# Last weight transposes moved to the score banks, and three low halves of the first expert's weights made by GpSimd

## The chip, the cores and the metric

The kernel runs on one core of one Trainium2 chip. The metric is the time of one execution on the device, in microseconds (us); lower is better.

## The reference

```python
def _attn_ref(q, k, v):              # q, k, v: (4, 8, 768, 64)
    block, window = (32, 16)
    k_sum = k.reshape(B, H, nb, block, D).max(axis=3)
    v_sum = v.reshape(B, H, nb, block, D).mean(axis=3)
    scores_l = scale * np.matmul(q, k.transpose(0, 1, 3, 2))
    mask_l = np.abs(pos[:, None] - pos[None, :]) < window
    scores_s = scale * np.einsum('bhsd,bhnd->bhsn', q, k_sum) + np.log(block)
    ...
    a = softmax over [masked local scores, block scores]
    return np.matmul(a, v_all)

def _moe_ref(x, w_group, w_expert, w1, w2):   # 3072 tokens of 512; 4 groups of 4 experts, hidden 1024
    g_idx = np.argmax(x @ w_group, axis=1)
    ...
        e_idx = np.argmax(xg @ w_expert[g], axis=1)
        ...
            h = np.maximum(xg[mask_e] @ w1[g, e], 0.0)
            ye = h @ w2[g, e]
            out[tok_idx] = combined[:, None] * ye
```

Local attention with block summaries is followed by a mixture of 16 experts, in which each token goes to one expert of one group.

## The kernel before

**Attention.** The 4 batches of 8 heads are 16 pairs of heads; each pair is cut into three groups of four blocks of 128 queries, which makes 48 groups (numbers 0 to 47 below). `attention()` steps through n = 0 to 50 and at each n issues, in the order that the table `PLAN` writes out, one piece of several groups at once: the scores of group n into two of the three score banks (`ps_s`), VectorE's masking and row minimum, ScalarE's exponentials ("e"), the transposes of the weights of group n - 2 (`transpose_p`, "t") with ScalarE's copy `ptS`, and the product with the values of group n - 3 (`values`, "v") into the one bank `ps_av`, which VectorE divides by the row sums into `x`. Steps "l0" to "l3" (`logits`) transpose x into `xT` and multiply it by the router's weights. Transposes of all kinds share the three banks `ps_tr` in turn.

**Routing.** `Router` works out which expert is largest and which of its tokens go first; its VectorE operations are fed into the stream between the others (`advance`). For the last batch but one they run at n = 48, in one piece: mx, dd, c, ..., seen. ScalarE takes one exponential, dd, from them.

**Experts.** Each product is made of three matmuls in a rounded fp32 format: high x high, low x high, high x low, where the high half is a rounding copy by ScalarE and the low half is a subtraction. `split_w` makes these halves of 128 x 1024 pieces; the four pieces (parts) of w1 of the first expert are split in the last steps of attention by `hook`. `hook` also gathers the first tokens (`gather1`), transposes them into high and low halves at n = 47 (`x_t1`), and advances `first`, whose stage 1 (`stage1_2`) writes hidden units into the score banks, two blocks of 128 to a bank; it takes two steps at n = 49 and one at n = 50 and n = 51, so stage 1 and the last steps of attention stand in each other's midst. Part p of w1 is first used by the p-th pair of hidden blocks.

Every engine runs its instructions in the order in which they were issued, GpSimd's queue with its gathers included. What is written out by hand here is that order: `SPLIT_AT` gives the step n, counted from 48, at which ScalarE's high half of each part is issued, and the low half follows one step later.

Of the kernel before, what the change touches and what calls it, by code (L numbers as in the profile page):

```python
# [8 lines left out]
F32 = mybir.dt.float32  # L9
# [5 lines left out]
ALU = mybir.AluOpType  # L15
# [40 lines left out]
T_LAG, V_LAG = 2, 3  # L56
# [6 lines left out]

W1_AT = 34
GATHER_AT, X_AT = 4, 1
SPLIT_AT = (-4, -3, -2, -1)
FIRST = {1: 2, 2: 1, 3: 1}

XT_AT = 4
# [5 lines left out]
class Banks:  # L75
# [5 lines left out]
    def next(self):  # L81
        self.n += 1
        return self.tiles[(self.n - 1) % len(self.tiles)]
# [506 lines left out]
def attention(tc, q, k, v, w_group, w_expert, ident, x_dram, ps, router, hook):  # L590
    nc = tc.nc
# [18 lines left out]
    V = nc.vector  # L610
    T = router.T
    ps_tr, ps_s, ps_av, ps_lg = ps["tr"], ps["s"], ps["av"], ps["lg"]
    lg = router.lg

    with ExitStack() as st, ExitStack() as nat_st:
# [6 lines left out]
        order = [(b, a) for b in range(B) for a in range(NP)]  # L622
# [36 lines left out]
        def keep_warm(n):  # L659
            t = ps_lg.next()  # L660
            for _ in range(n):
                nc.tensor.matmul(out=t, lhsT=zero, rhs=zero[:, None, :].broadcast_to([P, 4, P]), start=True, stop=True)  # L662
# [138 lines left out]
        def exps(n, sp, nm):  # L801
            pr = prr[n % 3]
            for i in range(4):
                nc.scalar.activation(out=pr[:, i, 0:NC], in_=sp[:, i], func=AF.Exp, bias=nm[:, i:i + 1], scale=-1.0)  # L804
            return pr

        def transpose_p(pr):
            pt = ps_tr.next()
            for i in range(4):
                T.transpose(out=pt[0:NR, i * P:(i + 1) * P], in_=pr[:, i], identity=ident)  # L810
            ptS = wk.tile([NR, 4, P], F32, name="ptS", bufs=3)
            nc.scalar.copy(out=ptS.rearrange("p a c -> p (a c)"), in_=pt[0:NR])
            return ptS
# [20 lines left out]
        def store():  # L834
            b, js = stores.pop(0)
            nc.sync.dma_start(out=x_dram[b * S:(b + 1) * S].rearrange("(j r) d -> r j d", r=P)[:, js], in_=xs[b][:, js])

        def logits(idx, part):
            b, a = order[idx]
            x = xs[b]  # L840
            if part < 2:
                if part == 0:
                    xTs[idx] = wk.tile([P, TB, P], F32, name="xT")
                j0, n = ((0, 4), (4, 2))[part]
                tp = ps_tr.next()
                for i in range(n):
                    T.transpose(out=tp[:, i * P:(i + 1) * P], in_=x[:, j0 + i, a * P:(a + 1) * P], identity=ident)
                (V.tensor_copy if part and idx < len(order) - 1 else nc.scalar.copy)(
                    out=xTs[idx][:, j0:j0 + n].rearrange("p c r -> p (c r)"), in_=tp[:, 0:n * P])
            elif part == 2:  # L850

                if a == 0:
                    lgp[b] = ps_lg.next()
                xT = xTs.pop(idx)
                for i in range(4):
                    rows = slice(32 * i, 32 * i + 32)
                    T.matmul(out=lgp[b][rows, 0:TB * 32], lhsT=wcat[:, a], rhs=xT[:, :, rows],
                             start=(a == 0), stop=(a == NP - 1), skip_group_check=True)
                if a == NP - 1:
                    lT = lgp["lT"] = sm.tile([P, TB * 32], F32, name="lT", bufs=1)  # L860
                    nc.scalar.copy(out=lT, in_=lgp.pop(b)[:, 0:TB * 32])
            elif a == NP - 1:
                tl = sm.tile([P, TB, 32], F32, name="tl", bufs=1)
                V.transpose(out=tl.rearrange("p t c -> p (t c)"), in_=lgp.pop("lT"))
                V.tensor_copy(out=lg[:, b * TB:(b + 1) * TB], in_=tl[:, :, 0:20])  # L865
                stores.extend((b, slice(j, j + 2)) for j in range(0, TB, 2))
# [4 lines left out]
        NG = 3 * len(order)  # L871
        prs, pts = {}, {}
# [14 lines left out]
        for n in range(NG + 3):  # L887
            idx, g = n // 3, n % 3
            if n < NG:
                b, a = order[idx]  # L890
                xs[b] = x_ring[b % 2]
            for step in START[n] if n < len(START) else PLAN[g]:
                if step == "s" and n < NG:
                    sps = scores(n)
                elif step == "e" and n < NG:
                    prs[n] = exps(n, *sps)
                elif step == "t" and 0 <= n - T_LAG < NG:
                    pts[n - T_LAG] = transpose_p(prs.pop(n - T_LAG))
                elif step == "v" and 0 <= n - V_LAG < NG:
                    values((n - V_LAG) // 3, (n - V_LAG) % 3, pts.pop(n - V_LAG))  # L900
                elif step[0] == "p" and n < NG and idx + 1 < len(order):
                    prep(idx + 1, int(step[1]))
                elif step[0] == "m" and n < NG:
                    j = idx + (step == "m0" and n > 2)
                    if (j > 0 or n < 3) and j < len(order):
                        means(j, int(step[1]))
                elif step == "w":
                    keep_warm(4)
                elif step == "n0":
                    means(1, 0)  # L910
                elif step[0] == "l" and 0 <= idx - LAG[step] < len(order):
                    logits(idx - LAG[step], int(step[1]))
            if n == 0:
                router.consts()
            elif n == 4:
                router.compared()
            if n in ROUTE_AT:
                b1 = ROUTE_AT.index(n)
                work.append(router.route(b1 * TB, (b1 + 1) * TB))
                if b1 == 1:  # L920
                    work.append(router.first_blocks())
            if n == NG - 4:
                nat_st.close()
            if n < NG:
                if g == 0 and idx + 2 < len(order):
                    load_vw(idx + 2)
                if g == 0 and idx < len(order) - 3:
                    qk[idx + 3] = load_qk(idx + 3)
            if g == 1 and stores:
                store()  # L930
            while stores and n == NG - 5:
                store()
            clock.step += 1
            hook(n, need, advance, w1_first)
# [11 lines left out]
class Experts:  # L946
# [76 lines left out]
    def split_w(self, row, which, parts, low=True, high=True):  # L1023

        raw = self.raw(row, which)
        for c in parts:
            js = slice(2 * c, 2 * c + 2)
            if which == 0:
                src = raw.rearrange("p c (j r) -> p c j r", j=FC)[:, :, js]
                h, l = (t[:, :, js] for t in self.w1s)  # L1030
            else:
                src = raw[:, js]
                h, l = (t[:, js] for t in self.w2s)
            if high:
                self.nc.scalar.copy(out=h, in_=src)  # L1035
            if low:
                self.V.tensor_tensor(out=l, in0=src, in1=h.bitcast(F32), op=ALU.subtract)

    def gather(self, row, dst, half=0):
        name, c = self.col(row, half)  # L1040
# [299 lines left out]
def block_attention_then_moe(tc, q, k, v, w_group, w_expert, w1, w2, out):  # L1340
    nc = tc.nc
    with ExitStack() as st:
# [12 lines left out]
        last = 3 * B * NP  # L1355

        first = ex.first()

        def hook(n, need, advance, space):

            if not ex.w1r and n >= W1_AT and (router.ready & 1 or n == last - 4):
                need(1)
                ex.w1r["first"] = space
                ex.load_w(("first", 0), 0)
            if n == last - 4:
                ex.tiles(st.enter_context(tc.tile_pool(name="m_w", bufs=1, side="right")), True)
            if n == last - GATHER_AT:
                need(2)
                ex.gather1(0)
                ex.load_w(("first", 0), 1, queue=nc.gpsimd)  # L1370
            if n == last - X_AT:
                ex.x_t1()
                if NE > 2:
                    ex.gather1(2)
            for part in range(4):
                if n == last + SPLIT_AT[part] + 1:
                    ex.split_w(("first", 0), 0, [part], high=False)
                if n == last + SPLIT_AT[part]:
                    ex.split_w(("first", 0), 0, [part], low=False)
            if n == last:  # L1380
                router.ahead = LATE_AHEAD
                advance(99)
            for _ in range(FIRST.get(n - last, 0)):
                next(first)
            if n > last + 1:
                advance(2 if n == last + 2 else 99)
# [3 lines left out]
        late = st.enter_context(tc.tile_pool(name="m_late", bufs=1))  # L1390
# [58 lines left out]
```

## Time and profile before

| | |
|---|---|
| median of 3 runs | 517.19 us (516.53 to 517.81) |
| profiled execution, own time | 515.85 us |
| its span, first to last instruction | 514.2 us |
| busy: TensorE matmul (PE) | 492.2 us, 96% |
| busy: TensorE weight load (PEld) | 415.5 us, 81% |
| busy: VectorE (DVE) | 356.6 us, 69% |
| busy: ScalarE (ACT) | 317.8 us, 62% |
| busy: GpSimd (POOL) | 120.9 us, 24% |

The profile is of one execution; its times count from the span's start. Busy shares are means over the whole span, and the seam that the change works on is only some 15 us of it, so the table says little of it: the rows below do.

### The profile page before, as it was taken

How to read it: one execution, taken by the hardware profiler on the slowest of the kernel's cores; microseconds unless marked ns; L12 is line 12 of the kernel's file. 1: busy time of each engine (PE TensorE's matmuls, PEld its weight loads, DVE VectorE, ACT ScalarE, POOL GpSimd, SP SyncE). 2: the span in 40 equal slices, each digit the busy share in tenths (PEclk: the TensorE clock that was granted, in tenths of full speed). 3: DMA queues.
4: the chain of work that ended last, by engine and by line, in shares of the span. 5: the costliest groups of instructions: out<-in, count | busy, mean ns of one | idle time of the engine just before them, and what ended most of it. 6: DMA issues, size and time to landing. Idle time of an engine off the chain costs nothing.

```text
span 514.2 us, 13346 instructions
## 1 busy us (share of the span) xinstructions
PE 492.2 (96%) x4974; PEld 415.5 (81%) x4974; DVE 356.6 (69%) x1084; ACT 317.8 (62%) x597; POOL 120.9 (24%) x205
## 2 busy tenths in 40 slices
PE   8999999999999899999999999999999999999994
PEld 4677767776777698979898989898898989897773
DVE  6687899888977978878755647483836556473773
ACT  5699888888988643216644556473645546474682
POOL 6122112211312600037020203022121202022332
PEclk9799999999999899999999999999999999999998
DMA  9999676879646820069997665665566756754891
GB/s 179 176 181 198 130 168 189 180 155 195 173 113 224 281 90 22 28 220 354 409 403 273 238 229 211 247 225 190 205 211 239 263 212 222 258 191 137 300 359 42
DMA packets 75316, 106.94 MB, mean 208 GB/s; under 512 B 40286, under 2 KB 40366, under 8 KB 75232
## 3 DMA queue, kind: packets, MB, share of 16 engines
q1 hardware_dynamic: 69184, 86.78, 58.5%
q0 software_dynamic: 6048, 19.12, 10.4%
q8 instruction: 43, 0.70, 0.6%
q14 instruction: 41, 0.34, 0.2%
HBM read 97.49 MB, written 13.24 MB: 215 GB/s over the span
## 4 chain that ended last, share of the span: by engine, by line
PE 49%; issue 19%; DMA 12%; DVE 11%; ACT 3%; POOL 3%; POOLq 1%; DVEq 0%; ACTq 0%
PE ps_s L122 26%; DMA out_dram<-y,t_unit_scatter 12%; PE ps_tr L122 12%; PE ps_av L122 10%; DVE ss L795 3%; DVE ks L775 2%; DVE kw L764 1%; ACT kw L764 1%; PE ps_lg L122 1%; POOL ohr L1042 1%; ACT qt L758 1%; PE ps_lg L662 1%; POOLq L1185 1%; ACT pr L804 1%; DVE kw L778 1%
## 5 line engine op out<-in xcount | busy, mean ns | idle before, releaser
L122 DVE TENSOR_TENSOR w2l<-w2r,w2h 128x1024 fp32r<-128x1024 f32 x52 | 63.4, 1225 | 77.1 <-ACT w2h L1035 76.6
L122 PE MATMUL ps_s<-xT,w1h 128*128 128x256 f32 x448 | 83.5, 284 | 0.0
L122 PEld LDWEIGHTS ps_s<-xT,w1h 128*128 128x128 f32 x448 | 70.7, 192 | 1.0 <-issue 0.7
L1082 POOL DMA_INDIRECT out_dram<-y,t_unit_scatter x24 | 25.7, 1069 | 190.9 <-ACT y L1077 97.7
L738 POOL COPY va<-vr 25x256 f32<-25x256 f32 x96 | 35.9, 418 | 118.8 <-DVE vr L735 118.8
L122 PE MATMUL ps_s<-xT,w1l 128*128 128x256 f32 x224 | 63.4, 283 | 0.0
L122 DVE TENSOR_TENSOR w1l<-w1r,w1h 128x1024 fp32r<-128x1024 f32 x52 | 60.4, 1219 | 3.6 <-ACT w1h L1035 3.6
L804 ACT ACTIVATE pr<-ss,nm 128x120 f32<-128x120 f32 x192 | 60.1, 387 | 3.3 <-DVE nm L795 2.9
L1120 ACT ACTIVATE hTh<-ps_s 128x512 fp32r<-128x512 f32 x48 | 28.7, 598 | 53.9 <-PE ps_s L122 31.9
L122 PE MATMUL ps_s<-ohr,w1h 128*128 128x256 f32 x320 | 58.9, 282 | 0.0
L1035 ACT CAST w2h<-w2r 128x1024 fp32r<-128x1024 f32 x52 | 53.8, 1041 | 1.5 <-DVE lg L865 0.9
L1035 ACT CAST w1h<-w1r 128x1024 fp32r<-128x1024 f32 x52 | 50.7, 1051 | 0.4 <-DMA w1r<-in_moe_w_dram 0.4
L122 PEld LDWEIGHTS ps_s<-ohr,w1h 128*128 128x128 f32 x320 | 49.8, 188 | 0.2
L122 DVE SCALAR_TENSOR_TENSOR hTl<-ps_s,hTh 128x512 fp32r<-128x512 f32 x48 | 33.2, 691 | 24.2 <-ACT hTh L1120 21.5
L795 DVE CUSTOM_DVE_ANT_0 ss<-mask,ps_s 128x120 f32<-128x120 f32 x192 | 42.1, 275 | 6.1 <-PE ps_s L122 4.6
L122 PE MATMUL ps_s<-ohr,w1l 128*128 128x256 f32 x160 | 45.0, 281 | 0.0
L122 PEld LDWEIGHTS ps_s<-xT,w1l 128*128 128x128 f32 x224 | 42.9, 192 | 0.3
L122 PE MATMUL ps_s<-kw,qt 64*64 64x120 f32 x768 | 37.5, 282 | 5.7 <-DVE nm L795 4.6
L122 PE MATMUL ps_s<-w2h,hTh 128*128 128x512 f32 x104 | 41.6, 400 | 0.0
L122 PE MATMUL ps_av<-w2h,hTh 128*128 128x512 f32 x104 | 41.6, 400 | 0.0
L122 PE MATMUL ps_av<-w2l,hTh 128*128 128x512 f32 x104 | 41.1, 395 | 0.0
L122 PE MATMUL ps_s<-w2h,hTl 128*128 128x512 f32 x104 | 41.1, 395 | 0.0
(275 smaller groups left out, 1010.6 us busy)
## 6 DMA issues: line engine op xcount, KB each, us to landing
w1r<-in_moe_w_dram SPq DMA_DIRECT2D x30, 1024.0 KB, 8.4
w2r<-in_moe_w_dram SPq DMA_DIRECT2D x28, 1024.0 KB, 5.6
kn<-in_k_dram SPq DMA_DIRECT2D x16, 384.0 KB, 4.5
qn<-in_q_dram SPq DMA_DIRECT2D x16, 384.0 KB, 5.4
va<-in_v_dram SPq DMA_DIRECT2D x32, 192.0 KB, 5.0
x_dram<-xt SPq DMA_DIRECT2D x12, 512.0 KB, 5.4
w2r<-in_moe_w_dram POOLq DMA_DIRECT2D x4, 1024.0 KB
va<-in_v_dram SPq DMA_DIRECT2D x64, 44.0 KB, 4.6
```

Source lines behind the costliest of these rows:

```text
L122: return f(*args, **kw)
L662: nc.tensor.matmul(out=t, lhsT=zero, rhs=zero[:, None, :].broadcast_to([P, 4, P]), start=True, stop=True)
L738: nc.gpsimd.tensor_copy(out=va[KW:NR, i:i + n, :, 0:D], in_=vr[KW:NR].broadcast_to([NBLK + 1, n, 2, D]))
L758: nc.scalar.activation(out=out[:, j], in_=tv.rearrange("p i t r -> p t i r"), func=AF.Copy, scale=-1.0 / 8.0)
L764: (nc.scalar.copy if j == 0 or h and idx in ACT_K1 else V.tensor_copy)(out=out[:, j], in_=tv.rearrange("p i t r -> p t r i"))
L775: V.reduce_max(out=ks, axis=AX.X, in_=kw[:, :, 0:QT].rearrange("p t (a k) -> p t a k", k=BLOCK))
L778: V.tensor_copy(out=kw[:, :, KW:NC], in_=ks[:, None, :].broadcast_to([P, NQT, NBLK]))
L795: V.tensor_tensor_reduce(out=ss[:, u], in0=mask[:, 1 if t == 0 else 2 if t == NQT - 2 else 0], in1=sp[h][:, j], scale=1.0, scalar=3.4e38, ...
L804: nc.scalar.activation(out=pr[:, i, 0:NC], in_=sp[:, i], func=AF.Exp, bias=nm[:, i:i + 1], scale=-1.0)
L1035: self.nc.scalar.copy(out=h, in_=src)
L1082: self.nc.gpsimd.indirect_dma_start(out=self.out, out_offset=bass.IndirectOffsetOnAxis(ap=self.tabs[name, "scatter"][0:y.shape[0], col:col ...
L1120: nc.scalar.activation(out=th[:, js], in_=hp, func=AF.Relu)
```

## The change

The transposes of groups 46 and 47 (n = 48 and 49) no longer take the next `ps_tr` bank but the first and the third score bank. The second x transposes of the last pair but one are copied out by ScalarE instead of VectorE. The high half of part 3 is issued one step later. The low half of part 0 stays on VectorE; those of parts 1 to 3 go to GpSimd and are issued at n = 49.

```diff
-SPLIT_AT = (-4, -3, -2, -1)
+SPLIT_AT = (-4, -3, -2, 0)
+LOW_AT = (-3, 1, 1, 1)
...
-        def transpose_p(pr):
-            pt = ps_tr.next()
+        def transpose_p(pr, late):
+            pt = ps_s.tiles[2 * late - 2] if late > 0 else ps_tr.next()
...
-                (V.tensor_copy if part and idx < len(order) - 1 else nc.scalar.copy)(
+                (V.tensor_copy if part and idx < len(order) - 2 else nc.scalar.copy)(
...
-                    pts[n - T_LAG] = transpose_p(prs.pop(n - T_LAG))
+                    pts[n - T_LAG] = transpose_p(prs.pop(n - T_LAG), n - NG + 1)
...
-                self.V.tensor_tensor(out=l, in0=src, in1=h.bitcast(F32), op=ALU.subtract)
+                eng = self.nc.gpsimd if row[0] == "first" and which == 0 and c else self.V
+                eng.tensor_tensor(out=l, in0=src, in1=h.bitcast(F32), op=ALU.subtract)
...
-                if n == last + SPLIT_AT[part] + 1:
+                if n == last + LOW_AT[part]:
                     ex.split_w(("first", 0), 0, [part], high=False)
```

On TensorE, from the transposes of the first tokens (xg, n = 47) to the start of stage 1, before:

```order
L122 MATMUL ps_tr_64<-identr,xg_3099 128x128 x4
L122 MATMUL ps_tr_65<-identr,xg_3100 128x128 x4
L122 MATMUL ps_tr_63<-ident,xt_114 128x128 x2
L122 MATMUL ps_tr_64<-ident,pr_192 121x128 x4
L122 MATMUL ps_av_69<-va_112,ptS 64x65 x8
L122 MATMUL ps_tr_65<-ident,pr_193 121x128 x4
L122 MATMUL ps_av_69<-va_112,ptS 64x65 x8
L122 MATMUL ps_lg_70<-xT,wcat 32x192 x4
L122 MATMUL ps_s_66<-xT_3101,w1h_3097 128x256
L122 MATMUL ps_s_66<-xT_3101,w1l_3098 128x256
```

and after (pr_192 and pr_193 are the weights of groups 46 and 47; 63 to 65 are the `ps_tr` banks, 66 to 68 the score banks):

```order
L123 MATMUL ps_tr_64<-identr,xg_3099 128x128 x4
L123 MATMUL ps_tr_65<-identr,xg_3100 128x128 x4
L123 MATMUL ps_tr_63<-ident,xt_114 128x128 x2
L123 MATMUL ps_s_66<-ident,pr_192 121x128 x4
L123 MATMUL ps_av_69<-va_112,ptS 64x65 x8
L123 MATMUL ps_s_68<-ident,pr_193 121x128 x4
L123 MATMUL ps_av_69<-va_112,ptS 64x65 x8
L123 MATMUL ps_lg_70<-xT,wcat 32x192 x4
L123 MATMUL ps_s_66<-xT_3101,w1h_3097 128x256
L123 MATMUL ps_s_66<-xT_3101,w1l_3098 128x256
```

The order is the same; pr_192 no longer takes the bank of xg_3099, and pr_193 no longer that of xg_3100. Stage 1 begins in bank 66, which pr_192 now uses before it.

On VectorE, behind the low halves of the first tokens (xT_3101) and into the routing of the last batch but one (mx, dd), before:

```order
L122 TENSOR_TENSOR w1l_3098<-w_first,w1h_3097 128x4x256
L848 COPY xT<-ps_tr_63 128x256
L826 RECIPROCAL rs<-ps_av_69 128x4
L827 TENSOR_TENSOR xt_114<-ps_av_69,rs 128x2x128
L122 TENSOR_SCALAR jb_first<-t_first_gather 128x4
L122 TENSOR_SCALAR hi_first<-t_first_gather 128x4
L122 TENSOR_TENSOR w1l_3098<-w_first,w1h_3097 128x4x256
L122 TENSOR_TENSOR lo_first<-jb_first,lo_first 128x4
L122 TENSOR_TENSOR hi_first<-hi_first,lo_first 128x4
L122 ISA t_first_scatter<-hi_first,em_first 128x8
L122 TENSOR_REDUCE mx_6_3323<-lg 128x30
L122 TENSOR_TENSOR dd_3325<-lg,mx_6_3323 128x120
```

and after, from the second low half of the tokens on:

```order
L123 TENSOR_TENSOR xT_3101<-ps_tr_65,xT_3101 128x4x128
L827 RECIPROCAL rs<-ps_av_69 128x4
L828 TENSOR_TENSOR xt_114<-ps_av_69,rs 128x2x128
L123 TENSOR_SCALAR jb_first<-t_first_gather 128x4
L123 TENSOR_SCALAR hi_first<-t_first_gather 128x4
L123 TENSOR_TENSOR lo_first<-jb_first,lo_first 128x4
L123 TENSOR_TENSOR hi_first<-hi_first,lo_first 128x4
L123 ISA t_first_scatter<-hi_first,em_first 128x8
L123 TENSOR_REDUCE mx_6_3320<-lg 128x30
L123 TENSOR_TENSOR dd_3322<-lg,mx_6_3320 128x120
```

Two low halves of w1 and the copy of xT are gone from here (a third low half stood ahead of the last masked scores); what is left keeps its order.

On GpSimd, from the last copies of the block means to the first outputs, after:

```order
L739 COPY va_112<-vr 25x4x64 x6
L1044 DMA xg_3099<-x_dram,t_first_gather 128x512
L1044 DMA xg_3100<-x_dram,t_first_gather 128x512
L1039 TENSOR_TENSOR w1l_3098<-w_first,w1h_3097 128x4x256 x3
L1084 DMA out_dram<-y_3492,t_first_scatter 3072x512
L1084 DMA out_dram<-y_3491,t_first_scatter 3072x512
```

The three subtractions (TENSOR_TENSOR) are new; they stand behind both gathers and ahead of the first expert's outputs.

## Rows read from the trace of the kernel before

**Rows 1.** Page, 40 slices of 12.86 us: granted TensorE clock, in tenths.
```profile
PEclk9799999999999899999999999999999999999998
```

**Rows 2.** Windows: length, then busy of PE, PEld, DVE, ACT, POOL; PEclk; DMA; GB/s.
```profile
172.00:176.00 4.00, 2.11 (x20) 1.56 (x20) 3.35 (x16) 3.68 (x9) 3.32 (x8) 1.00 0.99 333
176.00:180.00 4.00, 4.00 (x47) 3.10 (x46) 3.86 (x12) 0.54 (x1) 0.61 (x1) 0.57 0.88 303
```

**Rows 3.** Timeline, TensorE: start us, us, engine, line, operation, count, [idle before <- releaser].
```profile
172.89 0.89 PE L122 MATMUL ps_tr<-identr,xg 128*128 128x128 f32 x8 [0.69 <-DVE sc_first L122]
173.61 0.41 PE L122 MATMUL ps_tr<-ident,xt 128*128 128x128 f32 x2
...
175.22 0.70 PE L122 MATMUL ps_tr<-ident,pr 128*121 128x128 f32 x4 [1.20 <-DVE xT L122]
176.81 1.21 PE L122 MATMUL ps_tr<-ident,pr 128*121 128x128 f32 x4
177.95 1.14 PE L122 MATMUL ps_av<-va,ptS 121*64 121x65 f32 x16
179.01 0.70 PE L122 MATMUL ps_lg<-xT,wcat 128*32 128x192 f32 x8
179.65 0.38 PE L122 MATMUL ps_s<-xT,w1h 128*128 128x256 f32 x1
...
182.70 0.69 PE L122 MATMUL ps_av<-va,ptS 121*64 121x65 f32 x16
...
186.31 0.53 PE L122 MATMUL ps_lg<-xT,wcat 128*32 128x192 f32 x8 [0.46 <-ACT xT L848]
```

**Rows 4.** Timeline, ScalarE, 172.7 to 181.2 us.
```profile
172.72 1.25 ACT L804 ACTIVATE pr<-ss,nm 128x120 f32<-128x120 f32 x4
173.87 1.05 ACT L1054 CAST xT<-ps_tr 128x512 fp32r<-128x512 f32 x2
...
180.37 0.30 ACT L275 ACTIVATE dd<-dd 128x120 f32<-128x120 f32 x1 [3.83 <-DVE c L122]
180.58 0.57 ACT L812 COPY ptS<-ps_tr 121x512 f32<-121x512 f32 x1
```

**Rows 5.** Timeline, VectorE, 172.6 to 182.4 us.
```profile
172.67 0.16 DVE L122 COPY sc_first<-ps_tr 128x8 f32<-128x8 f32 x1
...
174.47 1.29 DVE L122 TENSOR_TENSOR xT<-ps_tr,xT 128x512 fp32r<-128x512 f32 x2 [0.61 <-ACT xT L1054]
...
177.14 0.17 DVE L826 RECIPROCAL rs<-ps_av 128x4 f32<-128x4 f32 x1
...
177.69 0.16 DVE L122 TENSOR_SCALAR jb_first<-t_first_gather 128x4 int32<-128x4 int32 x1
...
178.96 0.15 DVE L122 TENSOR_TENSOR lo_first<-jb_first,lo_first 128x4 int32<-128x4 int32 x1
...
180.05 0.28 DVE L122 SCALAR_TENSOR_TENSOR c<-dd,iom 128x120 f32<-128x120 f32 x1
...
181.96 0.42 DVE L827 TENSOR_TENSOR xt<-ps_av,rs 128x256 f32<-128x256 f32 x1
```

**Rows 6.** Timeline, GpSimd and VectorE side by side, twice.
```profile
170.64 1.45 POOL L738 COPY va<-vr 25x256 f32<-25x256 f32 x1 [1.08 <-DVE vr L735]
170.61 1.23 DVE L122 TENSOR_TENSOR w1l<-w_first,w1h 128x1024 fp32r<-128x1024 f32 x1
...
173.42 0.40 POOL L738 COPY va<-vr 25x256 f32<-25x256 f32 x1
173.41 0.44 DVE L122 TENSOR_SCALAR lo_first<-t_first_gather 128x4 int32<-128x4 int32 x1
```

**Rows 7.** Timeline, GpSimd: a wider copy, and the two gathers of first tokens.
```profile
6.05 0.28 POOL L706 COPY mask<-mask 128x120 f32<-128x120 f32 x1
...
174.20 1.09 POOL L1042 DMA_INDIRECT xg<-x_dram,t_first_gather  x1 [0.38 <-POOL va L738]
175.59 1.01 POOL L1042 DMA_INDIRECT xg<-x_dram,t_first_gather  x1 [0.30 <-issue]
```

## The prediction

> **What bounds the kernel now.** I read the page first. TensorE has matmul work in nearly all of the span, so a change counts only where it removes or adds a wait of TensorE. The strip of granted clock is at 8 or 9 nearly everywhere and shows two dips to 7 or 8: one at the start, one in the slice from 167 to 180 us [rows 1]. That second dip is where the change works: the seam at which attention ends and the first expert begins. Cut into 4 us windows, 172 to 176 us holds only 2.11 us of matmul, and the next window runs at a mean granted clock of 0.57, that is at the lower of the two levels (1.2 GHz) for (1 - 0.57) / 0.5 = 86% of it, some 3.4 us [rows 2].
>
> The timeline of TensorE tells why. The last x2 transposes before it end at 172.20 us, then it idles 0.69 us for VectorE's sc_first, does twelve transposes until 174.02, and idles 1.20 us until VectorE has made the low half of the first tokens, because the transposes of group 46's weights want the bank that this low half is read from [rows 3]. From 176 us the same work is slow: four transposes take 1.21 us where they took 0.70, and the logits product 0.70 where a later one takes 0.53 [rows 3]. Stage 1 of the first expert starts at 179.65, runs 24 matmuls, and at 182.70 comes the value product of group 47 [rows 3]. That product is released by two chains: ScalarE's exp of dd (behind VectorE's c) and then the copy ptS [rows 4], and VectorE's normalising of group 46, which stands behind the whole first part of the routing and ends at 181.96 + 0.42 = 182.38 [rows 5]. So VectorE is only 0.3 us early there: it is hidden now, and late as soon as it loses more.
>
> **What the score banks give.** In the changed order nothing but the score banks is wanted by the two last weight transposes, and both banks were read by 172.7, when the last scores were masked. VectorE also loses the low half at 170.61 (1.23 us) [rows 6], so sc_first, now at 172.67 [rows 5], comes some 1.2 us earlier and the 0.69 us wait goes. I rebuild TensorE: token transposes from 172.20 for 173.61 - 172.89 = 0.72 us; two x transposes 0.4, to 173.35; group 46's transposes 0.65 and group 45's value product 0.65, to 174.6; group 47's transposes to 175.2 (its exponentials end at 172.72 + 1.25 = 173.97 [rows 4]). Then one wait is left: the single value bank. VectorE must divide group 45 first, and stands at the low halves of the tokens, which follow ScalarE's casts (end 174.92 [rows 4]) and end at 174.47 + 1.29 = 175.76; the division takes 177.69 - 177.14 = 0.55 [rows 5]. So group 46's value product starts at about 176.25 and takes 0.65, the logits product 0.5, and stage 1 starts at 177.4 instead of 179.65: **2.25 us earlier**. Of this 0.9 us is idle time (0.69 + 1.20 gone, about 1.0 new) and some 1.35 us is clock, as the half clock cost (1.21 - 0.70) + (1.14 - 0.69) + (0.70 - 0.53) = 1.1 us on three rows and the rest on one more value product. The copy moved to ScalarE (0.4 us) stands ahead of group 46's ptS and ends both by 175.8, before the value bank is free: nothing.
>
> **What the three low halves cost.** VectorE loses three subtractions of 1.2 us; GpSimd gets three. Its queue holds six copies, the two gathers, and then the three. The copies were held up by VectorE: the one at 170.64 lasted 1.45 us, the others 0.40 [rows 6], so they now end 1.05 us earlier, at 172.77; the gathers (1.09, a pause of 0.30, 1.01, after a pause of 0.38 [rows 7]) then end at about 175.55, and the first subtraction starts at **175.7**.
>
> No row shows a subtraction on GpSimd. Its copies give the bounds: 0.28 us for 120 columns [rows 7] and 0.40 for 256 [rows 6] make 0.88 ns a column and 0.17 us fixed, so 1024 columns read once are 1.07 us. That is the low end; scaling the 0.40 by columns and by two inputs gives 3.2 us, the high end. I take 2.0 us (0.17 + 2 x 0.90, two inputs read one after the other), since the copy is the nearest work. The Trainium skill, GPSIMD Engine Reference, section 3.1, gives 4497 ns for 2048 columns of a two-input fp32 operation; half of that, an estimate of 2.25 us, would make my sum below 0.75 us longer.
>
> GpSimd's results are needed late: the second part at the second pair of hidden blocks, 183.95 us before. TensorE does not wait for them. The cost is on VectorE. Rows 6 show the two engines excluding each other, both ways: the copy at 170.64 ends 0.25 us after VectorE's subtraction does, and lo_first, four columns, lasts 0.44 us against 0.16 for its like jb [rows 5], and ends with the copy beside it [rows 6]. VectorE's operations from PSUM and its reductions show no such lengthening; those with two SBUF inputs, and small copies and scalar operations within SBUF, do.
>
> The rows show this for 0.4 us of GpSimd at a time; since each hold they show ends with the instruction that holds, I extend it to a long subtraction, and leave the other case, a hold in pieces, to the rivals. The Trainium skill, SBUF — State Buffer, section "Who interferes with whom", says that the shared pair of ports is held for the whole instruction and the other engine fully blocks; by that, an operation of VectorE could wait 2 us. The rows agree as far as they go, and no run here shows a longer one.
>
> So from 175.7 the chain jb, hi, lo, hi, scatter, dd, c, each with two SBUF inputs or of lo_first's kind, meets three subtractions back to back. A small one slips in between two of them (jb, hi or lo); the rest runs after the third, at 175.7 + 3 x 2.0 = 181.7. From lo to the end of c were 180.05 + 0.28 - 178.96 = 1.37 us, from there to the normalised group 46 another 182.38 - 180.33 = 2.05 [rows 5], and 0.1 to TensorE. Group 47's value product starts at 181.7 + 3.5 = **185.2** instead of 182.70: 2.5 us late. TensorE itself arrives at 177.4 + 3.05 = 180.45 and idles 4.75 us, more than the 1.9 us that dropped the clock before, so I add one more stretch like that one: 3.4 us at 1.2 GHz lose 1.7 us. Behind that value product queue the rank matmuls, the last x transposes and the rest of stage 1; from there TensorE is dense, so the delay reaches the end.
>
> **Sum.** 2.5 + 1.7 = +4.2 us. The profiled execution took 515.85 us (span 514.2) and would take 520.05; against the median of the runs, 517.19, it gives **521.4**. With 1.07 us a subtraction, the product starts at 175.7 + 3.2 + 3.5 = 182.4: -0.3, or +1.4 with the clock. With 3.2 us it starts at 188.8: +6.1 + 1.7 = +7.8, 525.0.
>
> **The rivals.** First, faster: GpSimd's long subtraction does not hold VectorE for its whole length, or only for parts. Then c is in time, nothing stands against the 2.25 us, and the kernel takes 514.9. For it: the rows show only short holds. Against: each hold shown lasts as long as the instruction. It decides if VectorE is held less than about 1.2 us in all, since the product may start at 180.45 and needs 175.7 + 3.5 = 179.2 without any hold. Second, no change: subtractions near 1.1 us, so that the hold gives back what the banks gained (516.9 to 518.6); or the hold is absent but the 1.0 us wait for the value bank keeps the clock low, and only 0.9 us is won (516.3). For it: 1.07 us is GpSimd's own pace for one input. Against: there are two. Third, the score banks become a wait of their own, stage 1 waiting in the first of them for ptS of group 46: that copy is done at 175.8, 1.6 us early, so I price it at nothing.
>
> **Chances.** Slower through the hold 0.62; faster 0.24; about the same 0.14. Changes within 0.3% (1.6 us) can't be told from none. The slower case alone spans 518.8 to 525; the range reaches down to the gain, 515.0 to 525.0, and leaves half of the faster case and the longest holds outside.
>
> **What would show it.** In the changed profile: no wait of TensorE on VectorE's xT at the weight transposes; stage 1 starting near 177.4; three subtractions on GpSimd from about 175.7, each some 2 us; VectorE's lo, dd or c lengthened to the ends of these; a gap of 4 to 5 us on TensorE ahead of the last value product, and a second dip of the clock. I am wrong if VectorE's rows keep their lengths beside GpSimd's, or if GpSimd starts after c.

## The result, and the profile after

The changed kernel takes **523.42 us** (median of 6 runs, 521.57 to 526.52) beside 517.27 us of the kernel before on the same chip (6 runs, 516.53 to 518.93): a ratio of 1.0114, 95% interval 1.0081 to 1.0146, that is 4.2 to 7.6 us slower. 521.4 was predicted. The profiled execution took 521.73 us, with a span of 520.0.

The strip of granted clock (in tenths, 40 slices of 13.0 us) has lost the dip at the start that [rows 1] show, and keeps the one at the seam:

```profile
PEclk9999999999999979999999999999999999999997
```

Windows of the seam after the change (columns as in [rows 2]):

```profile
176.00:180.00 4.00, 3.18 (x28) 2.94 (x24) 3.97 (x3) 0.00 (x0) 4.00 (x3) 1.00 0.81 281
180.00:184.00 4.00, 0.00 (x0) 0.00 (x0) 3.83 (x10) 0.78 (x2) 2.23 (x1) 0.76 0.02 8
184.00:188.00 4.00, 3.14 (x31) 3.04 (x32) 1.64 (x8) 0.54 (x2) 0.00 (x0) 0.50 0.47 173
```

From 180 to 184 us TensorE does nothing at all, and the four microseconds behind that run wholly at the lower level (0.50, 1.2 GHz). TensorE's timeline, which answers to [rows 3]:

```profile
171.66 0.60 PE L123 MATMUL ps_s<-ident,pr 128*121 128x128 f32 x4
...
174.97 0.69 PE L123 MATMUL ps_av<-va,ptS 121*64 121x65 f32 x16 [1.46 <-DVE xt L828]
175.58 0.53 PE L123 MATMUL ps_lg<-xT,wcat 128*32 128x192 f32 x8
176.04 0.39 PE L123 MATMUL ps_s<-xT,w1h 128*128 128x256 f32 x1
...
184.86 1.14 PE L123 MATMUL ps_av<-va,ptS 121*64 121x65 f32 x16 [5.68 <-DVE xt L828]
...
190.24 0.53 PE L123 MATMUL ps_lg<-xT,wcat 128*32 128x192 f32 x8 [0.46 <-ACT xT L849]
```

The 0.69 and 1.20 us waits of before are gone, a wait of 1.46 us for the value bank is new, and stage 1 starts early, at 176.04. Then group 47's value product waits 5.68 us for VectorE's xt, the normalised group 46. GpSimd, and the spread of its new instructions (ns, least, median, most):

```profile
170.32 2.14 POOL L739 COPY va<-vr 25x256 f32<-25x256 f32 x6 [0.91 <-DMA xg<-x_dram,t_first_gather]
172.73 1.09 POOL L1044 DMA_INDIRECT xg<-x_dram,t_first_gather  x1 [0.27 <-POOL va L739]
...
175.21 7.01 POOL L1039 TENSOR_TENSOR w1l<-w_first,w1h 128x1024 fp32r<-128x1024 f32 x3
```

```profile
L1039 POOL TENSOR_TENSOR w1l<-w_first,w1h x3: 2337/2377/2382, 175.2 to 179.9; 128x1024 fp32r<-128x1024 f32 x3
```

VectorE beside it (of before: [rows 5]):

```profile
174.74 0.38 DVE L123 TENSOR_SCALAR jb_first<-t_first_gather 128x4 int32<-128x4 int32 x1
...
175.35 2.27 DVE L123 TENSOR_TENSOR hi_first<-hi_first,lo_first 128x4 int32<-128x4 int32 x1
177.65 2.30 DVE L123 CUSTOM_DVE_ANT_0 t_first_scatter<-hi_first,em_first 128x8 uint16<-128x8 uint16 x1
179.87 0.26 DVE L123 TENSOR_REDUCE mx<-lg 128x30 f32<-128x120 f32 x1
180.17 2.19 DVE L123 TENSOR_TENSOR dd<-lg,mx 128x120 f32<-128x120 f32 x1
182.40 0.28 DVE L123 SCALAR_TENSOR_TENSOR c<-dd,iom 128x120 f32<-128x120 f32 x1
...
184.29 0.42 DVE L828 TENSOR_TENSOR xt<-ps_av,rs 128x256 f32<-128x256 f32 x1
```

Three operations on 4, 8 and 120 columns last 2.2 to 2.3 us, one to each subtraction of GpSimd; the reduction between them (mx) keeps its 0.26. The 0.38 of jb ends at 175.12, with GpSimd's second gather (174.13 + 1.01 = 175.14): it too seems to have held an operation. VectorE reads as 99% busy in the window from 176 us while it gets almost nothing done.

To compare executions I count from a mark ahead of the seam, a logits product of five matmuls near 157 us, so that an early clock dip, which only some executions have, falls out. The second mark is behind the seam: the transposes of the first tokens gathered by the units (xd). Before, and then after:

```profile
157.96 0.53 PE L122 MATMUL ps_lg<-xT,wcat 128*32 128x192 f32 x5
...
231.43 0.80 PE L122 MATMUL ps_tr<-identr,xd 128*128 128x128 f32 x8
```

```profile
156.85 0.53 PE L123 MATMUL ps_lg<-xT,wcat 128*32 128x192 f32 x5
...
235.35 0.79 PE L123 MATMUL ps_tr<-identr,xd 128*128 128x128 f32 x8
```

From the first mark to the last logits product are 186.31 - 157.96 = 28.35 us before and 190.24 - 156.85 = 33.39 after, so the seam costs **+5.04 us**; to the xd transposes 73.47 and 78.50, so the 5.03 us stay. The profiled span is 5.8 us longer: +5.03, less 1.11 that this execution was early at the first mark, and 1.74 more in the last scatter to the output, which ends the chain that ended last; 0.1 is left over (before, then after):

```profile
505.40 3.20 DMA out_dram<-y,t_unit_scatter
```

```profile
509.41 4.94 DMA out_dram<-y,t_unit_scatter
```

In the experiments' profiles that transfer takes 2.92 to 3.42 us, so I don't put the 1.74 down to the change.

### The profile page after: what moved, and what is told of

Read it like the earlier page. It is cut to its first block, busy times and chain, and to the rows that moved or that the text cites. A ratio compares the mean times of both kernels' runs of the same rounds, so it can differ in the third digit from the quotient of the medians.

```text
span 520.0 us, 13347 instructions
## 1 busy us (share of the span) xinstructions
PE 488.7 (94%) x4974; PEld 413.4 (79%) x4974; DVE 359.3 (69%) x1080; ACT 317.5 (61%) x598; POOL 127.7 (25%) x208
## 5 line engine op out<-in xcount | busy, mean ns | idle before, releaser
L123 PE MATMUL ps_s<-w2l,hTh 128*128 128x512 f32 x104 | 41.1, 395 | 0.0
```

Source lines behind the costliest of these rows:

```text
L123: return f(*args, **kw)
```

## The experiments

The theory: a long GpSimd instruction holds VectorE's operations with two SBUF inputs, and its small one-input ones within SBUF, till its own end, one held operation to each instruction; the routing of the last batch but one, and with it group 47's value product, comes late by the sum. The rivals: TensorE or VectorE waits for the results of GpSimd; the score banks do the harm; the long transfer of work as such costs, wherever it stands. Each kernel was timed against the kernel before on the same chip (median 516.2 us in the first four, 516.5 in the others). In the table, "wait" is the idle time of TensorE ahead of group 47's value product, and the next two columns are the times from the first mark to the last logits product and to the xd transposes, less 28.35 and 73.47, in one profiled execution each. Where that execution lies off the median, these columns do too: it took 518.23 us for kernel 1, 522.04 for kernel 2 and 514.23 for kernel 7.

| kernel | wait, us | logits, us | xd, us | median, us | ratio to before |
|---|---|---|---|---|---|
| the change | 5.68 | +5.04 | +5.03 | 523.42 | 1.0114 (1.0081 to 1.0146) |
| 1 banks alone | 0 | +0.98 | +0.98 | 516.46 | 1.0002 (0.9978 to 1.0026) |
| 2 GpSimd alone | 4.41 | +5.76 | +6.67 | 520.97 | 1.0090 (1.0056 to 1.0124) |
| 3 lows late on VectorE | 0 | -2.07 | +0.39 | 515.18 | 0.9978 (0.9953 to 1.0003) |
| 4 subtractions in 12 | 2.20 | +3.40 | +3.34 | 518.78 | 1.0072 (1.0045 to 1.0100) |
| 5 read by nobody | 3.74 | +3.17 | +3.36 | 519.46 | 1.0087 (1.0058 to 1.0115) |
| 6 fills | 0.16 | -1.61 | -0.23 | 514.97 | 0.9978 (0.9959 to 0.9997) |
| 7 behind seen | 0 | -1.98 | +0.11 | 515.99 | 1.0006 (0.9984 to 1.0028) |
| 8 one on GpSimd | 1.05 | -0.92 | +0.29 | 515.58 | 1.0004 (0.9982 to 1.0026) |

**1. The score banks alone**, on the kernel before.

```diff
-        def transpose_p(pr):
-            pt = ps_tr.next()
+        def transpose_p(pr, late):
+            pt = ps_s.tiles[2 * late - 2] if late > 0 else ps_tr.next()
...
```

> The score banks alone, all low halves on VectorE where they were. Theory (the score banks pay only once VectorE is unloaded): the transposes of group 46 no longer wait, but group 46's value product still needs VectorE's division of group 45, which stands behind the tokens' low halves, one low half of w1 (1.22 us) and a copy, at about 177.8 us, so stage 1 starts 0 to 0.3 us earlier than 179.65 and the time is 516.5 to 517.4, no change. Rival (the banks are the whole gain of the change): stage 1 starts 2 us or more earlier and the time is about 515.

No change in the time; stage 1 starts 181.42 - 159.47 = 21.95 us behind the first mark where it was 21.69. TensorE and VectorE of this kernel:

```profile
179.58 1.11 PE L122 MATMUL ps_av<-va,ptS 121*64 121x65 f32 x16 [1.83 <-DVE hi_first L122]
```

```profile
177.34 1.21 DVE L122 TENSOR_TENSOR w1l<-w_first,w1h 128x1024 fp32r<-128x1024 f32 x1
178.47 0.42 DVE L848 COPY xT<-ps_tr 128x256 f32<-128x256 f32 x1
```

The wait for the bank is replaced by one for the value bank, because VectorE's low half and copy stand ahead of the division. The profile names hi_first, which ends at that moment; the division of group 45 ends at 179.43, the 0.15 us ahead that lie between xt and the product in the change too (174.82 to 174.97). The product that waited is at the lower clock (1.11 us for 0.69). By the median the banks neither harm nor help by themselves.

**2. The GpSimd subtractions alone**, from the change with the old banks.

```diff
-            pt = ps_s.tiles[2 * late - 2] if late > 0 else ps_tr.next()
+            pt = ps_tr.next()
```

> The three low halves on GpSimd as in the change, but the last weight transposes in their old banks. Theory (VectorE held by GpSimd's subtractions is the whole loss): the product of group 47 comes as late as in the change or some 0.5 us later, since VectorE reaches its chain later and meets the same three subtractions; the time is 522.5 to 524.5, as with the whole change. Rival (the new use of the score banks costs, for example a wait of stage 1 in them): without the banks the loss goes, and the time is 515 to 518.

Slower by 0.9%: the loss belongs to the subtractions. The median, 520.97, lies below the 522.5 to 524.5 expected, and above the 515 to 518 of the rival. GpSimd spends 7.03 us on the subtractions from 174.90, VectorE's lo_first lasts 2.31 us and the second hi_first 2.28. VectorE and TensorE of this kernel:

```profile
177.32 2.31 DVE L123 TENSOR_TENSOR lo_first<-jb_first,lo_first 128x4 int32<-128x4 int32 x1
```

```profile
185.14 1.14 PE L123 MATMUL ps_av<-va,ptS 121*64 121x65 f32 x16 [4.41 <-DVE xt L828]
```

**3. The whole change, but the low halves on VectorE**, parts 2 and 3 behind the routing.

```diff
-LOW_AT = (-3, 1, 1, 1)
+LOW_AT = (-3, 1, 2, 2)
...
-                eng = self.nc.gpsimd if row[0] == "first" and which == 0 and c else self.V
+                eng = self.V
```

> The whole change, but the three low halves are made by VectorE, one at n = 49 and two at n = 50, behind the routing. Theory: the banks' gain stays and nothing holds VectorE, stage 1 starts 2.2 to 2.5 us earlier than before, the product of group 47 has no gap ahead of it, and the time is 514.5 to 515.5. Rival (issuing the low halves late is what costs, whoever makes them): the first late low half is waited for, and the time is 518 or more.

The loss is gone. Stage 1 starts 2.07 us sooner than before (176.55 - 156.93 = 19.62 us behind the first mark against 21.69), a little less than the 2.2 to 2.5 expected. VectorE of this kernel:

```profile
175.24 0.16 DVE L123 TENSOR_SCALAR jb_first<-t_first_gather 128x4 int32<-128x4 int32 x1
...
176.53 0.28 DVE L123 SCALAR_TENSOR_TENSOR c<-dd,iom 128x120 f32<-128x120 f32 x1
...
178.43 0.42 DVE L828 TENSOR_TENSOR xt<-ps_av,rs 128x256 f32<-128x256 f32 x1
```

From jb to c are 1.57 us where the change took 7.94 (174.74 to 182.68), and xt is done before TensorE wants it.

**4. The three subtractions cut into twelve** of 256 columns.

```diff
-                eng.tensor_tensor(out=l, in0=src, in1=h.bitcast(F32), op=ALU.subtract)
...
+                else:
+                    for kc in range(KC):
+                        eng.tensor_tensor(out=l[:, kc], in0=src[:, kc], in1=h[:, kc].bitcast(F32), op=ALU.subtract)
```

> The whole change, with each of GpSimd's three subtractions cut into four of 256 columns, about 0.6 us each. Theory (a hold lasts as long as one GpSimd instruction, and VectorE gets one operation in between two of them): no VectorE operation lasts more than about 0.8 us where 2.2 to 2.3 us were seen, the routing's first part ends 2 to 2.5 us earlier than in the change, and the time is 518.5 to 521. Rival 1 (what counts is when the last subtraction ends): no better than the change, 523 or more. Rival 2 (TensorE waits for GpSimd's low halves themselves): no better either, and the gap's end moves with the subtractions.

Shorter holds, but more of them. GpSimd's tile, two rows of VectorE, and one of TensorE:

```profile
L1043 POOL TENSOR_TENSOR w1l<-w_first,w1h x12: 719/730/774, 175.0 to 182.7; 128x256 fp32r<-128x256 f32 x12
```

```profile
175.81 0.65 DVE L123 TENSOR_TENSOR lo_first<-jb_first,lo_first 128x4 int32<-128x4 int32 x1
...
182.92 0.42 DVE L828 TENSOR_TENSOR xt<-ps_av,rs 128x256 f32<-128x256 f32 x1
```

```profile
183.49 1.07 PE L123 MATMUL ps_av<-va,ptS 121*64 121x65 f32 x16 [2.20 <-POOL w1l L1043]
```

Eleven operations of VectorE, from jb to seen, are lengthened by 0.1 to 0.55 us, 4.5 us in all; in the change it was three by 1.9 to 2.1 us, 6.2 in all. The loss is only a third smaller, and the twelve take 8.42 us of GpSimd where the three took 7.01. The first part of the routing (to seen) ends 1.4 us sooner than in the change, counted from the first mark, and not the 2 to 2.5 expected. Here the profile names GpSimd's last piece, which ends at 175.03 + 8.42 = 183.45, for the end of TensorE's wait; xt ends at 183.34, the usual 0.15 us ahead of the product. That TensorE did not wait for GpSimd's results is seen from the two ends: from the first mark, GpSimd is done 1.2 us later than in the change (26.58 us behind it against 25.37), and the product starts 1.4 us sooner (26.62 against 28.01).

**5. Kernel 3, and beside it three GpSimd subtractions that nobody reads.**

```diff
+            if n == last + 1:
+                for part in (1, 2, 3):
+                    src = ex.w1r["first"].rearrange("p c (j r) -> p c j r", j=FC)[:, :, 2 * part:2 * part + 2]
+                    dst = ex.hT2[1][:, 4:8].rearrange("p c (j r) -> p c j r", j=2)
+                    nc.gpsimd.tensor_tensor(out=dst, in0=src, in1=src, op=ALU.subtract)
```

> The version with the three low halves on VectorE again (which took 0.998 of the time before), and beside it, at the place of the change, three GpSimd subtractions of the same size whose results nobody reads; all products stay what they were. Theory (each GpSimd subtraction holds VectorE's routing operations to its end): the routing chain is stretched as in the change, one operation per subtraction, the value product of group 47 waits till about 184.5 to 185.5, TensorE idles 4 to 6 us, and the time is that of the change or a little more, since VectorE has the three low halves to make as well: ratio 1.008 to 1.018. Rival (the loss comes from TensorE or VectorE waiting for GpSimd's results, the low halves themselves): nothing waits for these results, so the ratio stays at 0.995 to 1.001.

The loss comes back. GpSimd, VectorE and TensorE of this kernel:

```profile
175.43 5.85 POOL L1386 TENSOR_TENSOR hTl<-w_first 128x1024 fp32r<-128x1024 f32 x3
```

```profile
175.72 1.62 DVE L123 TENSOR_SCALAR jb_first<-t_first_gather 128x4 int32<-128x4 int32 x1
...
177.58 1.75 DVE L123 TENSOR_TENSOR hi_first<-hi_first,lo_first 128x4 int32<-128x4 int32 x1
...
179.74 1.68 DVE L123 TENSOR_TENSOR dd<-lg,mx 128x120 f32<-128x120 f32 x1
```

```profile
183.91 0.69 PE L123 MATMUL ps_av<-va,ptS 121*64 121x65 f32 x16 [3.74 <-DVE xt L828]
```

Nothing uses these results, and the last of them is there at 175.43 + 5.85 = 181.28, 2.6 us ahead of the product, so the rival of a wait for data falls. The product starts earlier than expected (184.5 to 185.5), and the wait is shorter than the 4 to 6 us expected: a subtraction that reads one tensor twice took 1.90 us here and not 2.36, 1.4 us less for three.

**6. Kernel 3, and beside it seven GpSimd fills** of 128 x 1024.

```diff
+FILLS = 7
...
+            if n == last + 1:
+                for _ in range(FILLS):
+                    nc.gpsimd.memset(ex.hT2[1][:, 4:8].bitcast(F32), 0.0)
```

> The same version with the low halves on VectorE, and beside it seven GpSimd fills of 128 x 1024 in place of the subtractions: instructions that write SBUF and read nothing, about 1 us each by the profile's fills (0.2 us for 128 columns), 7 us in all. If a GpSimd instruction of any kind holds VectorE to its own end, seven of the routing operations are held for about 1 us each, the chain to c ends some 5 us later, and the ratio is 1.006 to 1.015. If GpSimd must read SBUF to hold VectorE, the routing runs as if alone and the ratio is 0.995 to 1.001. I lean to the first, 60 to 40.

My lean was wrong: no loss. GpSimd, VectorE and TensorE:

```profile
175.19 7.02 POOL L1385 MEMSET hTl<- 128x1024 f32 x7
```

```profile
171.73 0.40 DVE L124 TENSOR_TENSOR t_first_weight<-sc_first 128x4 f32<-128x4 f32 x1
...
175.53 0.65 DVE L124 TENSOR_SCALAR jb_first<-t_first_gather 128x4 int32<-128x4 int32 x1
...
176.98 0.28 DVE L124 TENSOR_TENSOR dd<-lg,mx 128x120 f32<-128x120 f32 x1
...
178.42 0.78 DVE L124 CAST sb<-seen 128x16 bf16<-128x16 f32 x1
```

```profile
180.14 0.69 PE L124 MATMUL ps_av<-va,ptS 121*64 121x65 f32 x16 [0.16 <-DVE xt L829]
```

GpSimd is as busy as in the change (7.02 us against 7.01) and at the same place, but dd, with two SBUF inputs, keeps its 0.28 us. Only one-input operations within SBUF are held, jb and hi to 176.18 and the cast sb, with what stands right behind it, to 179.20, which are the ends of the first and the fourth fill (steps of 1.00 us from 175.19). In the same run t_first_weight, a VectorE addition with two SBUF inputs, lasts 0.40 us where it took 0.19 before; it stands beside GpSimd's copies, which read SBUF. So it is not GpSimd's time alone that counts, but what its instructions do with SBUF. That agrees with the Trainium skill, SBUF — State Buffer, section "Who interferes with whom": a VectorE instruction with two SBUF inputs contends with a GpSimd instruction that reads SBUF and not with one that only writes it, while copies, casts and tensor_scalar can run in a two-port mode, in which they contend with GpSimd.

**7. The change, with the subtractions behind seen**, the last result of the routing but the ranks: a small GpSimd copy reads it first.

```diff
-LOW_AT = (-3, 1, 1, 1)
+LOW_AT = (-3, 2, 2, 2)
...
+            if n == last + 2:
+                nc.gpsimd.tensor_copy(out=ex.hT2[1][:, 4, 0:16], in_=router.seen)
```

> The whole change, with GpSimd's three subtractions behind a small copy of the last result of the routing (seen), so that they start at about 178.4 instead of 175.2. Theory (it is the meeting with the routing that costs, not the subtractions as such): routing and normalising of group 46 run unheld, the value product of group 47 does not wait, and the ratio is 0.994 to 1.002; parts 1 to 3 are made by 180.9, 183.3 and 185.7, the first of them just in time for the second pair of hidden blocks. Rival (long GpSimd work costs the same wherever it stands, because the hidden units' low halves and the later routing on VectorE are held instead): 1.005 to 1.012.

The loss is gone with the whole 7.06 us of subtractions still on GpSimd. GpSimd, VectorE and TensorE:

```profile
177.94 0.20 POOL L1378 CAST hTl<-seen 128x16 fp32r<-128x16 f32 x1 [3.68 <-DVE seen L123]
178.11 7.06 POOL L1039 TENSOR_TENSOR w1l<-w_first,w1h 128x1024 fp32r<-128x1024 f32 x3
```

```profile
178.00 0.42 DVE L828 TENSOR_TENSOR xt<-ps_av,rs 128x256 f32<-128x256 f32 x1
...
182.92 2.48 DVE L123 TENSOR_SCALAR ri<-ri 128x6 int32<-128x6 int32 x2
```

```profile
189.11 0.39 PE L123 MATMUL ps_s<-xT,w1h 128*128 128x256 f32 x1 [1.28 <-DVE hTl L123]
```

xt is in time, as the theory has it. But one operation is held: the pair of ri operations, six columns wide, takes 2.48 us where kernel 3 needs 0.38. The low half of hidden units some way behind it is late, and TensorE waits 1.28 us for that where kernel 3 waits 0.43. The rival has a part of the truth: a later place has its own bill, though at the xd transposes kernel 7 is not behind kernel 3 for it (+0.11 and +0.39).

**8. One subtraction on GpSimd**, two on VectorE behind the routing.

```diff
-LOW_AT = (-3, 1, 1, 1)
+LOW_AT = (-3, 1, 2, 2)
...
-                eng = self.nc.gpsimd if row[0] == "first" and which == 0 and c else self.V
+                eng = self.nc.gpsimd if row[0] == "first" and which == 0 and c == 1 else self.V
```

> The change with only part 1 on GpSimd, parts 2 and 3 on VectorE behind the routing. Theory (loss per subtraction, one VectorE operation held to the end of each): one subtraction ends at 177.5, lo to c takes 1.37 us more, the normalised group 46 another 2.05, so the value product starts at 181.0, where TensorE arrives at about 179.6: 1.4 us of wait, hardly any clock loss, and the ratio is 0.997 to 1.003, near no change. Rival (the loss is not proportional, a single held operation already drops the clock): 1.004 to 1.008.

One operation is held (jb, 1.90 us), the product starts at 180.75 where 181.0 was worked out, and TensorE waits 1.05 us:

```profile
180.75 0.69 PE L123 MATMUL ps_av<-va,ptS 121*64 121x65 f32 x16 [1.05 <-DVE xt L828]
```

**Where the gain of kernels 3, 6, 7 and 8 goes.** They pass the last logits product 0.9 to 2.1 us sooner than before, and at the xd transposes little or nothing is left of it. TensorE of kernel 3 shows new waits in between, for VectorE's low half of hidden units and for the routing of the last batch (eb):

```profile
188.68 0.38 PE L123 MATMUL ps_s<-xT,w1h 128*128 128x256 f32 x1 [0.43 <-DVE hTl L123]
...
198.55 0.20 PE L123 MATMUL ps_tr<-eb,tri 128*128 128x96 bf16 x1 [0.43 <-DVE eb L123]
```

Kernels 6, 7 and 8 wait at the same two places (0.59, 1.28 and 0.41 us, then 0.41 to 0.42). Before and after the change TensorE does not: there VectorE has the time. Kernel 3 is still 0.83 us ahead at the first product with bo_unit (217.50 - 156.93 = 60.57 beside 219.36 - 157.96 = 61.40) and loses the rest in a stretch from 224 to 232 us whose granted clock is 0.79 in this execution and 1.00 in that of before. Of the four only kernel 6 has an interval below 1, and that by 0.03%.

## Why the prediction was right

All times of after are here put 1.11 us later, to the mark of before.

- **Score banks.** Predicted: no wait of the weight transposes, 1.0 us of wait for the value bank, stage 1 at 177.4. Measured: no wait, 1.46 us, 176.04 + 1.11 = 177.15. Kernel 1 adds what I had said only in part: the gain needs VectorE to be rid of the low halves too, since the banks alone give nothing.
- **Start of the first subtraction.** Predicted 175.7, measured 175.21 + 1.11 = 176.32. The step "they now end 1.05 us earlier" failed by 0.8: GpSimd's copies ended at 172.46 + 1.11 = 173.57 and not 172.77, the profile naming a DMA as what released them and no longer VectorE's vr.
- **One subtraction.** 2.0 us estimated, 2.34 to 2.38 measured, so 7.01 us for three in place of 6.0. My pace for two inputs in turn was too quick. The Trainium skill's figure (GPSIMD Engine Reference, section 3.1), 4497 ns for 2048 columns, halved to an estimate of 2.25 us, was nearer and still low.
- **The hold.** Each subtraction held one operation for its whole length, as I extended it from rows of 0.4 us [rows 6]. Kernels 2 and 5 show that this needs neither the banks nor the data, kernel 6 that for two-input operations it needs GpSimd to read, which I had not said.
- **The chain behind it.** I had it run from lo on after the third subtraction, 3.5 us. In fact three operations got through, the last of them dd with the end of the third (180.17 + 2.19 = 182.36), so only c and what follows was left: 184.86 - 182.22 = 2.64 us. In sum the product starts at 185.97 and not 185.2: +0.62 + 1.01 - 0.86 = +0.77. Two errors went one way and the third the other, so that the start came within 0.8 us is in part luck.
- **The clock.** From the product to the last logits product are 5.38 us and were 3.61 [rows 3]: 1.77, predicted 1.7. In kernel 8, with 1.05 us of wait, it is 184.37 - 180.75 = 3.62, in kernel 5, with 3.74 us, 188.74 - 183.91 = 4.83, and in kernel 2, with 4.41 us, 191.15 - 185.14 = 6.01, more than in the change after a shorter wait. Kernel 4 lost clock already before its wait (0.60 granted from 176 to 180 us). So the loss does not follow from the length of one wait, and that 1.7 came out so close is in part luck; I had only carried over the loss of the stretch before.
- **The sum.** +4.2 predicted for the seam, 3.27 + 1.77 = +5.04 measured. The medians differ by more, 523.42 - 517.27 = 6.15 us, so 1.1 us of the loss is not shown at the seam. The profiled execution is the second shortest of the six, and the six spread over 5 us, with a mean granted clock from 0.987 in the shortest to 0.973 in the longest, which lies above my range. Why the clock differs between them stays open, and with it whether the 1.1 us belong to the mechanism.
- **The rival "faster"** seems wrong in its price too: with no hold I gave 514.9, a gain of 2.25 us. Kernel 3 has no hold and its median is 1.0 us below before's, an interval that reaches no change, since later waits for VectorE and what they slow down take 1.24 of its 2.07 us back. But there VectorE makes the low halves itself, and no kernel here has subtractions on GpSimd that hold nothing, so the price of this rival was not tested as such.

## What to carry to other kernels

Work handed to an engine that sits idle is not free if the two hold each other up in SBUF, as GpSimd and VectorE do here: look at what the busy engine does at that very place, and whether a short chain that others wait for runs there. Cutting the work small moves the cost to more holds; placing it behind the chain removes that cost, and then the next chain on that engine must be looked at as well. A gain at one seam counts only as far as the next engine behind it has time to spare, so read on for a few tens of microseconds behind the place before a price is put on it.

## What the runs showed of the hardware that I had not expected

- Beside GpSimd instructions that stand back to back, VectorE had about one held operation to each: three beside three subtractions (2.27, 2.30 and 2.19 us in the change), eleven beside twelve of 256 columns (0.65 us for lo). Reductions between them pass unheld (0.26 us), and in kernel 5 the first hi and lo get through behind jb (0.16 us each) before the next one is held.
- GpSimd fills of 1024 columns (0.95 us each) leave two-input operations of VectorE alone and hold its one-input ones (0.78 us for a cast of 16 columns that takes 0.17 elsewhere).
- A GpSimd subtraction of 1024 columns takes 2.34 to 2.38 us with two tensors read, and 1.90 us where both inputs are the same tensor. Why was not tried.
